# Moving the output matmuls, the convolution and the weight loads inside a fused conv and ELU-FFN kernel

## The chip, the cores and the metric

The kernel runs on one core of a Trainium2 chip. The metric is the device time of one execution in microseconds (us), and a time without further remark is the median of several executions. The kernel before took 735.51 us (three runs, 735.46 to 736.42).

All runs below gave the right result. Every one was labelled fast, but for e10_xcopy1, e11_rounds_only and e13_conv_only, which ran once only, so that their state is unknown. The kernel before falls into two groups, about 735.2 to 736.4 and 737.2 to 739.0.

## The reference

```python
# attention-like part: 8 heads of 24 channels, 7 causal taps, softmax over the taps
w = exp(weight - weight.max(-1)); w = w / (w.sum(-1) + 1e-9)          # (8, 7)
x_pad = concat([zeros(B, 6, D), x], axis=1)                            # x: (8, 4096, 192)
out[b, s, h, :] = sum_k w[h, k] * x_pad[b, s + k, h, :]
# feed-forward part on the 32768 tokens
h = out.reshape(32768, 192) @ moe_w_in                                 # (192, 2048)
g = where(h > 0, h, exp(min(h, 0)) - 1)                                # ELU
return g @ moe_w_out                                                   # (2048, 192), f32
```

Every fourth block of 1024 tokens starts a new sequence, and its convolution (conv) reads six rows of zeros in place of the six tokens before.

## The kernel before

The work is cut into 32 "supers" of 1024 tokens, and each super into 16 steps. TensorE is used as two half arrays ("tiles") of 64 rows, each with its own stream. In one step each tile computes three matmuls into one bank of PSUM (an "h", 512 columns each), and some output items (192 columns each), whose number per step stands in `ROUNDS`. Then ACT takes the exp of the bank into E, POOL clamps E to 0..1, and DVE computes gT = max(E - 1, h) and so frees the bank. Six banks form a ring. Conv of later supers takes banks of that ring too; two more banks ("ops") collect the output.

```python
ROUNDS = (
    ((0, (0, 20)), (1, (1, 7, 9, 7, 8)), (0, (12,))),
    ((0, (0, 15, 7, 10)), (1, (5, 8, 6, 13))),
)
WCOLS = ((0, 256), (256, 768), (768, 1280), (1280, 2048))      # chunks in which w_in is loaded
CONV_AT = ((4, 1, 1, 0), (10, 1, 1, 1), (12, 2, 0, 0), (15, 2, 0, 1))   # (step, supers ahead, group, half)
EARLY_CONV = ((6, 1, 0, 0), (7, 1, 0, 1), (8, 1, 1, 0), (9, 1, 1, 1), (11, 2, 0, 0), (12, 2, 0, 1))
X_PAD, X_COPY, X_LOAD = 8, 1, 15        # steps at which POOL pads, POOL copies x, SP loads xg
# ... cut ...
# PE, ahead of a conv group
if m == 0:
    W(s_tm, 1)                          # the tap matrix Tm is there
for part in range(2):
    x_ready(W, s, part)
W(s_z, z_need[s])                       # the zeros ahead of a new sequence are there
wait_bank()
# ... cut ...
# POOL: one stream, in order
load_w_in(0, (0, 1)); load_w_in(1, (0, 1)); load_x(1, 0); load_w_in(2, (0, 1))
load_x(1, 1); load_w_in(3, (0, 1)); load_x(2, 0); load_x(2, 1)
g.dma_start(w_out...)
for n in range(NP):
    s, i = divmod(n, NQ)
    if i == X_PAD and s + 2 < NS and (s + 2) % SPB == 0:
        pad_x(s + 2)                    # memset of six rows of xg
    if i == X_COPY and s and s + 3 < NS:
        copy_x(s + 3)
    if n == X_LATE[0]:
        copy_x(3)
    for u in range(2):
        W(s_exp, 2 * n + u + 1)
        g.tensor_scalar(E..., ALU.min, ALU.max)
# ... cut ...
# DVE, after its part of the setup and ahead of every gT
W(s_band, 48)                           # Tr, the band of taps, has landed
v.tensor_copy(Tm[:], Tr[:, :, ::-1]).then_inc(s_tm)
for x_, op in enumerate(steps):
    ...                                 # gT = max(E - 1, h)
```

Of the kernel before, what the change touches and what calls it, by code (L numbers as in the profile page):

```python
# [14 lines left out]
FC = 128  # L15
# [15 lines left out]
NG3 = 2  # L31
LAG = -4
ROUNDS = (
    ((0, (0, 20)), (1, (1, 7, 9, 7, 8)), (0, (12,))),
    ((0, (0, 15, 7, 10)), (1, (5, 8, 6, 13))),
)
WCOLS = ((0, 256), (256, 768), (768, 1280), (1280, 2048))
Q_PART = (0,) * 2 + (1,) * 4 + (2,) * 4 + (3,) * 6
WARM = (9, 1)

CONV_AT = ((4, 1, 1, 0), (10, 1, 1, 1), (12, 2, 0, 0), (15, 2, 0, 1))
EARLY_CONV = ((6, 1, 0, 0), (7, 1, 0, 1), (8, 1, 1, 0), (9, 1, 1, 1), (11, 2, 0, 0), (12, 2, 0, 1))
M_NS, R_NS, C_NS = 215.8, 82.5, 102.5
QUAD = 4
XTW = 136
HALO = 2
X_PAD, X_COPY, X_LOAD = 8, 1, 15
X_LATE = (13, 22)


def bass_lightweight_conv__then__act_elu_kernel(
# [37 lines left out]
    for t in range(NS):  # L89
        for half, stretches in enumerate(ROUNDS):  # L90
            n, at = NQ * (t + 1) + LAG + 8 * half, [0, 0]
            for turned, sizes in stretches:
                for size in sizes:
                    part = each[at[turned] : at[turned] + size]
                    at[turned] += size
                    rounds_at.setdefault(n, []).extend(
                        (t, half, q, kb, turned ^ (t % 2)) for q, kb in part
                    )
                    n += 1
            assert at == [len(each)] * 2  # L100
# [43 lines left out]
    for n in range(NP):  # L144
        s, i = divmod(n, NQ)
        convs = [(ahead, g, b) for at, ahead, g, b in EARLY_CONV if at == n]
        convs += [
            (s + ahead, g, b)
            for at, ahead, g, b in CONV_AT
            if at == i and s + ahead < NS  # L150
            and (s + ahead, g, b) not in [e[1:] for e in EARLY_CONV]
        ]
        for u in range(2):
            rt = 1 - u
            beside = [
                ("c", 2 * cs + g - 2, b, u, hh)
                for cs, g, b in convs
                for hh in range(HB)
            ]
            if n < first_round:  # L160
                beside += [("w", rt)] * WARM[1]
            beside += [single(item, rt) for item in rounds_at.get(n, ())]
            if rt and n in turns_at:
                beside.insert(0, ("h", n, 1, 0))
            put(u, [("h", n, u, j) for j in range(u and n in turns_at, 3)])
            put(rt, beside)
        if n % 2:
            at[:] = [max(at)] * 2
# [9 lines left out]
            left[acc_of(op)] = left.get(acc_of(op), 0) + 1  # L178
    for x_, op in enumerate(steps):
        if op[0] in "hc" and not any(op[3:]):  # L180
            take_bank(op[:3])
        elif op[0] == "o":
            acc = acc_of(op)
            if acc not in lastly:
                begins.add(x_)
                if acc[:2] == (last, 1):
                    take_bank(("l",) + acc)
            elif steps[lastly[acc]][2] != op[2]:
                ends_run[lastly[acc]] = 0
            lastly[acc] = x_  # L190
            left[acc] -= 1
            if not left[acc]:
                ends_run[x_] = 0
                final[acc] = x_
# [21 lines left out]
    with ExitStack() as stack:  # L216
# [35 lines left out]
        H = psum("H", [P, 3, 2 * GS])  # L252
        ops = psum("ops", [P, 2, GS])

        s_w = [sema(f"s_w{i}") for i in range(5)]
        s_wd = sema("s_wd")
        s_xl = [sema(f"s_xl{i}") for i in range(2)]
        s_xh = sema("s_xh")
# [67 lines left out]
            return H[:, (0, 2, 1)[j], GS * r : GS * r + GS // 2]  # L326

        def bank_of(what):
            k = turn_of[what]
            return H[:, k // 2, GS * (k % 2) : GS * (k % 2 + 1)]  # L330

# [55 lines left out]
        def _gpsimd(g: bass.BassGpSimd):  # L387
# [27 lines left out]
            def load_w_in(k, halves):  # L415
# [27 lines left out]
            load_w_in(0, (0, 1))  # L443
            load_w_in(1, (0, 1))
            load_x(1, 0)
            load_w_in(2, (0, 1))
            load_x(1, 1)
            load_w_in(3, (0, 1))
            load_x(2, 0)
            load_x(2, 1)  # L450
            g.dma_start(
                w_out.rearrange("p (q r) d -> p q (r d)", r=2), moe_w_out.rearrange("(q p r) d -> p q (r d)", p=FC, r=2)
            ).then_inc(s_w[4], 16)
            for n in range(NP):
                s, i = divmod(n, NQ)
                if i == X_PAD and s + 2 < NS and (s + 2) % SPB == 0:
# [158 lines left out]
        def _tensor(pe):  # L615
# [75 lines left out]
            for x_, op in enumerate(steps):  # L691
                if op[0] == "w":
                    rt = op[1]
                    pe.matmul(  # L694
                        ops[:, rt, :],
                        zw[HP * rt : HP * (rt + 1), 0:P],
                        zw[HP * rt : HP * (rt + 1), :],
                        start=True,
# [3 lines left out]
                elif op[0] == "c":  # L702
# [5 lines left out]
                    elif hh == 0:  # L708
                        if m == 0:
                            W(s_tm, 1)  # L710
                        for part in range(2):
                            x_ready(W, s, part)
                        W(s_z, z_need[s])
                        wait_bank()
                    n1 = BN // HB
                    h = 4 * u + HB * b + hh
                    ins = pe.matmul(  # L717
# [11 lines left out]
                elif op[0] == "h":  # L729
# [5 lines left out]
                    if j == 0:  # L735
# [5 lines left out]
                        w_in[  # L741
                            HP * r : HP * (r + 1),
                            j,
                            2 * FC * (q // 2) + q % 2 : 2 * FC * (q // 2 + 1) : 2,
                        ],
                        att[HP * r : HP * (r + 1), s % 2, j, 0:GS],
                        start=(j == 0),
# [5 lines left out]
                else:  # L753
                    _, item, rt, g = op
                    t, half, q, kb, turned = item
                    acc = acc_of(op)
                    W(s_w[4], 16)
                    W(s_tt, 2 * (NQ * t + q) + g + 1)
                    at_end = acc[:2] == (last, 1)
                    if x_ in begins:  # L760
                        if at_end:
                            wait_bank()
                        elif acc in previous:
                            taken(W, previous[acc])
                    elif steps[seen[acc]][2] != rt:
                        W(s_swap[1 - rt], ends_run[seen[acc]])
                    seen[acc] = x_
# [107 lines left out]
```

## Time and profile before

| | before |
|---|---|
| median of runs | 735.51 us |
| span of the profiled run, granted TensorE clock | 734.2 us, 1.000 |
| first h matmul of step 0 | 11.59 us |
| super 0, super 1 | 23.06, 22.48 us |
| one steady super (supers 3 to 28) | 22.25 us |
| work of one tile in a super | 21.74 us |

"Super to super" here and below is the distance between the starts of the first h matmul of two supers, read from the trace. A step starts with its first h matmul, counting six to a step in order of time. The prediction shows the totals, the waits and the windows of before; its windows, and those of after further down, were all set 0.31 us later than the steps that they are named for, which changes no length. Lines of a timeline give start us, us, engine, line, operation, [idle before and releaser]. This is the group of the conv matmuls (line, engine, operation, output<-inputs, shapes, count | busy us, mean ns | idle time of the engine just before, and its releaser):

```profile
L717 PE MATMUL H<-xg,Tm 64*128 64x240 bf16 x496 | 90.6, 263 | 1.1 <-DVE gT L605 1.1
```

Conv costs PE nearly no waiting in the kernel before. And this is DVE's timeline at the start (start us, us, engine, line, operation, [idle before and releaser]):

```profile
12.19 0.55 DVE L591 COPY Tm<-Tr 128x1024 bf16<-128x1024 bf16 x1
14.11 0.69 DVE L605 SCALAR_TENSOR_TENSOR gT<-E,H 128x512 f16<-128x512 f32 x1 [1.36 <-POOL E L464]
```

The copy of the tap matrix has no bracket: Tr had landed before DVE came to it. It is over before POOL hands DVE its first E.

### The profile page before, as it was taken

To read this page: it belongs to the slowest core of one execution; us is meant where nothing else is said; L and a number is where in the kernel's file an instruction comes from. 1 tells how busy PE (TensorE), PEld (TensorE's weight loads), DVE (VectorE), ACT (ScalarE), POOL (GpSimd) and SP (SyncE) were. 2 spreads that over 40 slices of the span, in tenths; PEclk is the share of its full clock that TensorE was granted. 3 is DMA by queue.
4 is the path that set the end of the run, shared out by engine and by line. 5 is a ranking of instruction groups with operands and counts; after the bars stand their busy time and mean duration, and the time that the engine had idled before them with its cause. 6 is when DMAs were issued, how large, how long until landed. Compare 5 with 4: busy or idle time off the path is not lost.

```text
span 734.2 us, 28751 instructions
## 1 busy us (share of the span) xinstructions
PE 726.9 (99%) x11878; PEld 653.8 (89%) x11878; DVE 655.4 (89%) x1044; ACT 675.9 (92%) x1286; POOL 637.4 (87%) x1080
## 2 busy tenths in 40 slices
PE   9899999999999999999999999999999999999998
PEld 4599899999989999999998999998998999899997
DVE  5899999999999899899999999999999999999995
ACT  5899999999999999999999999999999999999994
POOL 8889888889888888888898888898888898888894
PEclk9999999999999999999999999999999999999999
DMA  9742444333543424443424443334435334432112
GB/s 172 116 116 69 114 104 99 98 82 78 115 101 85 112 65 98 114 93 94 94 67 114 114 94 93 90 71 114 104 82 112 72 90 115 93 93 69 38 54 67
DMA packets 130303, 69.12 MB, mean 94 GB/s; under 512 B 93996, under 2 KB 129324, under 8 KB 129708
## 3 DMA queue, kind: packets, MB, share of 16 engines
q1 hardware_dynamic: 123596, 52.04, 26.9%
q0 software_dynamic: 6288, 14.75, 12.5%
q8 instruction: 93, 1.52, 0.9%
q10 hardware_dynamic: 288, 0.49, 0.2%
q14 instruction: 38, 0.31, 0.1%
HBM read 43.51 MB, written 36.57 MB: 109 GB/s over the span
## 4 chain that ended last, share of the span: by engine, by line
PE 95%; DVE 2%; POOL 1%; ACT 1%; issue 1%; ACTq 0%
PE ops L771 49%; PE H L739 41%; PE H L717 3%; DVE gT L605 2%; POOL E L464 1%; PE H L771 1%; PE ops L633 1%; ACT E L536 0%; PE H L677 0%; PE ops L677 0%; PE H L657 0%; ACT csb L514 0%; POOL x_cast L410 0%; PE H L644 0%; POOL x_cast L407 0%
## 5 line engine op out<-in xcount | busy, mean ns | idle before, releaser
L605 DVE SCALAR_TENSOR_TENSOR gT<-E,H 128x512 f16<-128x512 f32 x1024 | 649.1, 683 | 63.4 <-POOL E L464 53.0
L464 POOL TENSOR_SCALAR E<-E 128x512 f32<-128x512 f32 x1024 | 611.1, 616 | 85.5 <-ACT E L536 80.0
L739 PE MATMUL H<-att,w_in 64*128 64x512 bf16 x3072 | 633.2, 376 | 1.7 <-DVE gT L605 1.2
L536 ACT ACTIVATE E<-H 128x512 f32<-128x512 f32 x1024 | 587.4, 603 | 40.1 <-PE H L739 24.6
L771 PE MATMUL ops<-w_out,gT 64*128 64x192 f16 x8064 | 616.9, 243 | 0.0
L771 PEld LDWEIGHTS ops<-w_out,gT 64*128 64x128 f16 x8064 | 538.8, 94 | 18.4 <-PE ops L771 16.5
L739 PEld LDWEIGHTS H<-att,w_in 64*128 64x128 bf16 x3072 | 257.4, 94 | 37.1 <-DVE gT L605 14.5
L717 PE MATMUL H<-xg,Tm 64*128 64x240 bf16 x496 | 90.6, 263 | 1.1 <-DVE gT L605 1.1
L514 ACT ACTIVATE csb<-H 128x480 bf16<-128x480 f32 x124 | 72.9, 588 | 0.0
L506 ACT ACTIVATE osb<-ops 128x384 f32<-128x384 f32 x125 | 61.9, 495 | 7.3 <-PE ops L771 5.9
L717 PEld LDWEIGHTS H<-xg,Tm 64*128 64x128 bf16 x496 | 45.4, 93 | 15.9 <-issue 1.3
L410 POOL DMA_DIRECT2D x_cast<-in_x_dram x29 | 15.4, 530 | 0.0
L694 PE MATMUL ops<-zw 64*128 64x512 bf16 x24 | 8.8, 376 | 0.0
L771 PE MATMUL H<-w_out,gT 64*128 64x192 f16 x128 | 6.4, 243 | 0.0
L771 PEld LDWEIGHTS H<-w_out,gT 64*128 64x128 f16 x128 | 5.7, 94 | 0.0
L418 POOL DMA_DIRECT2D w_in<-in_moe_w_in_dram x8 | 5.2, 660 | 0.3 <-DMA wh<-in_weight_dram 0.3
L633 PE MATMUL ops<-zw 128*128 128x512 bf16 x9 | 4.0, 628 | 1.2 <-DVE zw L546 1.2
L597 DVE COPY osb<-ops 128x384 f32<-128x384 f32 x1 | 0.6, 557 | 4.2 <-PE ops L771 4.2
L633 PEld LDWEIGHTS ops<-zw 128*128 128x128 bf16 x9 | 1.2, 139 | 3.2 <-issue 2.0
L391 POOL DMA_DIRECT2D xg<-in_x_dram x4 | 3.9, 982 | 0.0
L582 DVE CAST att<-H 128x512 bf16<-128x512 f32 x1 | 0.7, 692 | 3.1 <-PE H L677 3.1
L677 PE MATMUL H<-xT,Dg 64*128 64x256 bf16 x32 | 2.6, 326 | 0.0
(47 smaller groups left out, 27.4 us busy)
## 6 DMA issues: line engine op xcount, KB each, us to landing
out_dram<-osb SPq DMA_DIRECT2D x126, 192.0 KB, 2.4
x_cast<-in_x_dram POOLq DMA_DIRECT2D x29, 384.0 KB, 4.6
xg<-x_cast SPq DMA_DIRECT2D x58, 192.0 KB
xg<-x_cast SPq DMA_DIRECT2D x58, 26.2 KB
xg<-in_x_dram POOLq DMA_DIRECT2D x4, 240.0 KB, 10.3
w_in<-in_moe_w_in_dram POOLq DMA_DIRECT2D x4, 192.0 KB, 6.5
w_out<-in_moe_w_out_dram POOLq DMA_DIRECT2D x1, 768.0 KB, 14.4
w_in<-in_moe_w_in_dram POOLq DMA_DIRECT2D x2, 288.0 KB, 10.0
```

The source lines that it names most:

```text
L410: g.dma_start(xb[s * SUP : (s + 1) * SUP, :].rearrange("(p t) d -> p (t d)", p=P), x_flat[s * SUP : (s + 1) * SUP, :].rearrange("(p t) d - ...
L418: g.dma_start(w_in[HP * r : HP * (r + 1), :, c0:c1], moe_w_in.rearrange("(p j) f -> p j f", j=3)[:, :, c0:c1],).then_inc(s_w[k], 16)
L464: g.tensor_scalar(out=E[:, n % NE, u, :], in0=E[:, n % NE, u, :], scalar1=1.0, scalar2=0.0, op0=ALU.min, op1=ALU.max,).then_inc(s_clp)
L506: a.activation(*out_pieces(acc), ACT.Copy).then_inc(s_oev)
L514: return a.activation(csb[:, s % 2, :].rearrange("p (j v h i) -> p h j v i", j=3, v=2 * WPG, h=HEADS)[:, h0 : h0 + HB], bank_of(("c", m, b ...
L536: a.activation(E[:, n % NE, u, :], bank_of(op[:3]), ACT.Exp).then_inc(s_exp)
L605: v.scalar_tensor_tensor(out=gT[:, s % NG3, q, u, :], in0=E[:, n % NE, u, :], scalar=1.0, in1=bank_of(op[:3]), op0=ALU.subtract, op1=ALU.m ...
L633: pe.matmul(ops[:, 0, :], zw[:, 0:P], zw[:], start=True, stop=True)
L694: pe.matmul(ops[:, rt, :], zw[HP * rt : HP * (rt + 1), 0:P], zw[HP * rt : HP * (rt + 1), :], start=True, stop=True, tile_position=(HP * rt ...
L717: ins = pe.matmul(bank_of(op[:3])[:, n1 * hh : n1 * (hh + 1)], Tm[HP * rt : HP * (rt + 1), h, :], xg[HP * rt : HP * (rt + 1), s % NXB, :, ...
L739: ins = pe.matmul(bank_of(op[:3]), w_in[HP * r : HP * (r + 1), j, 2 * FC * (q // 2) + q % 2 : 2 * FC * (q // 2 + 1) : 2,], att[HP * r : HP ...
L771: ins = pe.matmul(to[:, d0 : d0 + D], gT[HP * rt : HP * (rt + 1), t % NG3, q, g, t0 : t0 + P], w_out[HP * rt : HP * (rt + 1), q, :], start ...
```

## The change

The intent has four parts: other counts of output items per step and other stretches, so that fewer steps are short at the wrong place; conv and the copy of x at other steps; conv of super 1 in the two output banks, which are idle at the start, so that the ring keeps six banks; and w_in loaded in two chunks, with runs of 1 and 3 KB, in place of four chunks with runs of 0.5 to 1.5 KB, and w_out with longer runs and ahead of the x of super 2.

```diff
 ROUNDS = (
-    ((0, (0, 20)), (1, (1, 7, 9, 7, 8)), (0, (12,))),
-    ((0, (0, 15, 7, 10)), (1, (5, 8, 6, 13))),
+    ((0, (0, 11, 10)), (1, (10, 6, 6, 10)), (0, (11,))),
+    ((0, (0, 15, 8, 9)), (1, (6, 6, 7, 13))),
 )
-WCOLS = ((0, 256), (256, 768), (768, 1280), (1280, 2048))
-Q_PART = (0,) * 2 + (1,) * 4 + (2,) * 4 + (3,) * 6
+RUN = 4
+WCOLS = ((0, 512), (512, 2048))
+Q_PART = (0,) * 4 + (1,) * 12
-CONV_AT = ((4, 1, 1, 0), (10, 1, 1, 1), (12, 2, 0, 0), (15, 2, 0, 1))
-EARLY_CONV = ((6, 1, 0, 0), (7, 1, 0, 1), (8, 1, 1, 0), (9, 1, 1, 1), (11, 2, 0, 0), (12, 2, 0, 1))
+CONV_AT = ((0, 1, 1, 0), (4, 1, 1, 1), (9, 2, 0, 0), (12, 2, 0, 1))
+EARLY_CONV = ((7, 1, 0, 0), (8, 1, 0, 1), (9, 1, 1, 0), (10, 1, 1, 1), (13, 2, 0, 0), (14, 2, 0, 1))
+OPS_CONV = 2
-X_PAD, X_COPY, X_LOAD = 8, 1, 15
-X_LATE = (13, 22)
+X_PAD, X_COPY, X_LOAD = 8, 3, 15
+X_LATE = (13, 18)
@@ a conv of the first super takes no bank of the ring
-            take_bank(op[:3])
+            if op[0] == "h" or op[1] >= OPS_CONV:
+                take_bank(op[:3])
@@ bank_of
+            if what[0] == "c" and what[1] < OPS_CONV:
+                return ops[:, what[2], :]
@@ POOL, the loads
             load_w_in(0, (0, 1))
             load_w_in(1, (0, 1))
             load_x(1, 0)
-            load_w_in(2, (0, 1))
             load_x(1, 1)
-            load_w_in(3, (0, 1))
+            g.dma_start(w_out ..., r=RUN).then_inc(s_w[2], 16)
             load_x(2, 0)
             load_x(2, 1)
@@ PE, conv
-                        wait_bank()
+                        if m >= OPS_CONV:
+                            wait_bank()
+                        elif m:
+                            W(s_ce, 2 * (m - 1) + b + 1)
```

Cut: the semaphores' numbers, the stride with which PE reads w_in, the warming matmuls (6 steps in place of 12, and to the other output bank), one more wait of the second early conv, and the waits of the first output item on its bank.

More of the change, by code (lines that the diff above doesn't have):

```diff
@@ L33 @@
 ROUNDS = (
-    ((0, (0, 20)), (1, (1, 7, 9, 7, 8)), (0, (12,))),
-    ((0, (0, 15, 7, 10)), (1, (5, 8, 6, 13))),
-)
-WCOLS = ((0, 256), (256, 768), (768, 1280), (1280, 2048))
-Q_PART = (0,) * 2 + (1,) * 4 + (2,) * 4 + (3,) * 6
+    ((0, (0, 11, 10)), (1, (10, 6, 6, 10)), (0, (11,))),
+    ((0, (0, 15, 8, 9)), (1, (6, 6, 7, 13))),
+)
+RUN = 4
+WCOLS = ((0, 512), (512, 2048))
+Q_PART = (0,) * 4 + (1,) * 12
 WARM = (9, 1)
-CONV_AT = ((4, 1, 1, 0), (10, 1, 1, 1), (12, 2, 0, 0), (15, 2, 0, 1))
-EARLY_CONV = ((6, 1, 0, 0), (7, 1, 0, 1), (8, 1, 1, 0), (9, 1, 1, 1), (11, 2, 0, 0), (12, 2, 0, 1))
+CONV_AT = ((0, 1, 1, 0), (4, 1, 1, 1), (9, 2, 0, 0), (12, 2, 0, 1))
+EARLY_CONV = ((7, 1, 0, 0), (8, 1, 0, 1), (9, 1, 1, 0), (10, 1, 1, 1), (13, 2, 0, 0), (14, 2, 0, 1))
+OPS_CONV = 2
+FIRST = {}
 M_NS, R_NS, C_NS = 215.8, 82.5, 102.5
@@ L91, in bass_lightweight_conv__then__act_elu_kernel @@
             n, at = NQ * (t + 1) + LAG + 8 * half, [0, 0]
+            if t == 0 and half in FIRST:
+                n, stretches = FIRST[half]
             for turned, sizes in stretches:
@@ L159, in bass_lightweight_conv__then__act_elu_kernel @@
             ]
-            if n < first_round:
+            if n + 1 < EARLY_CONV[0][0]:
                 beside += [("w", rt)] * WARM[1]
@@ L253, in bass_lightweight_conv__then__act_elu_kernel @@
         ops = psum("ops", [P, 2, GS])
-        s_w = [sema(f"s_w{i}") for i in range(5)]
+        s_w = [sema(f"s_w{i}") for i in range(3)]
         s_wd = sema("s_wd")
@@ L445, in _gpsimd @@
             load_x(1, 0)
-            load_w_in(2, (0, 1))
             load_x(1, 1)
-            load_w_in(3, (0, 1))
+            g.dma_start(
+                w_out.rearrange("p (q r) d -> p q (r d)", r=RUN),
+                moe_w_out.rearrange("(q p r) d -> p q (r d)", p=FC, r=RUN),
+            ).then_inc(s_w[2], 16)
             load_x(2, 0)
             load_x(2, 1)
-            g.dma_start(
-                w_out.rearrange("p (q r) d -> p q (r d)", r=2), moe_w_out.rearrange("(q p r) d -> p q (r d)", p=FC, r=2)
-            ).then_inc(s_w[4], 16)
             for n in range(NP):
@@ L694, in _tensor @@
                     pe.matmul(
-                        ops[:, rt, :],
+                        ops[:, 1 - rt, :],
                         zw[HP * rt : HP * (rt + 1), 0:P],
@@ L710, in _tensor @@
                             W(s_tm, 1)
+                            if b:
+                                W(s_cv, 1)
                         for part in range(2):
@@ L743, in _tensor @@
                             j,
-                            2 * FC * (q // 2) + q % 2 : 2 * FC * (q // 2 + 1) : 2,
+                            RUN * FC * (q // RUN) + q % RUN : RUN * FC * (q // RUN + 1) : RUN,
                         ],
@@ L756, in _tensor @@
                     acc = acc_of(op)
-                    W(s_w[4], 16)
+                    W(s_w[2], 16)
                     W(s_tt, 2 * (NQ * t + q) + g + 1)
@@ L764, in _tensor @@
                             taken(W, previous[acc])
+                        else:
+                            W(s_ce, 2 * (OPS_CONV - 1) + g + 1)
                     elif steps[seen[acc]][2] != rt:
```

## The prediction

> **What bounds the kernel now.** I read the engine totals first, then the groups, then the waits, then windows cut at the kernel's own stages, and last the start times of the single matmuls in the trace. Engines, and the groups that make up their time (line, engine, operation, output<-inputs, shapes, count | busy us, mean ns | idle before, releaser):
>
> ```profile
> PE 726.9 (99%) x11878; PEld 653.8 (89%) x11878; DVE 655.4 (89%) x1044; ACT 675.9 (92%) x1286; POOL 637.4 (87%) x1080
> ...
> L605 DVE SCALAR_TENSOR_TENSOR gT<-E,H 128x512 f16<-128x512 f32 x1024 | 649.1, 683 | 63.4 <-POOL E L464 53.0
> L464 POOL TENSOR_SCALAR E<-E 128x512 f32<-128x512 f32 x1024 | 611.1, 616 | 85.5 <-ACT E L536 80.0
> L739 PE MATMUL H<-att,w_in 64*128 64x512 bf16 x3072 | 633.2, 376 | 1.7 <-DVE gT L605 1.2
> L536 ACT ACTIVATE E<-H 128x512 f32<-128x512 f32 x1024 | 587.4, 603 | 40.1 <-PE H L739 24.6
> L771 PE MATMUL ops<-w_out,gT 64*128 64x192 f16 x8064 | 616.9, 243 | 0.0
> ```
>
> PE looks full, but its matmuls use half the rows (64*128), so two streams ("tiles") run side by side and PE counts as busy when only one of them works. Idle time must be counted per tile. The weight loads show it: they stop while a tile cannot go on.
>
> ```profile
> PEld H L739 <- DVE gT L605: 14.5, 44, 0.7
> PEld H L739 <- issue: 9.6, 31, 0.4
> ```
>
> 31 times is once for each super of 1024 tokens but one, and DVE (gT) is what frees the H banks. So some 24 us lie in short, regular stops. The start times confirm it. On one tile, starts follow each other by 215.8 ns (h matmul, 512 columns), 82.5 ns (output matmul) and 102.5 ns (conv matmul). A super has 96, 256 and 16 of them, half on each tile: 48 x 215.8 + 128 x 82.5 + 8 x 102.5 = 21.74 us. The trace takes 22.25 us from super to super (supers 3 to 28). Each tile loses 0.51 us. Placing every matmul on its tile, in program order, the loss sits in few places: at step 0 of the 16 steps (tile 0 idle 0.26, tile 1 0.16 just before it), at step 4 (0.25 and 0.18), and 0.06 on tile 1 at each of the three places where the output runs swap tiles.
>
> The start is different. Windows: steps 0 to 5 of super 0, steps 6 to 12, steps 13 to 15, then two steady supers (us; then PE, PEld, DVE, ACT, POOL busy with counts, clock, DMA share, GB/s):
>
> ```profile
> 11.90:18.84 6.94, 6.61 (x49) 2.12 (x45) 5.58 (x10) 6.06 (x13) 5.97 (x11) 1.00 1.30 193
> 18.84:30.70 11.86, 9.73 (x84) 4.08 (x85) 10.02 (x17) 9.76 (x21) 8.90 (x15) 1.00 0.86 136
> 30.70:34.96 4.26, 4.26 (x79) 4.05 (x76) 3.04 (x5) 3.54 (x8) 4.07 (x8) 1.00 0.59 95
> 235.47:257.73 22.26, 22.25 (x373) 20.28 (x369) 20.35 (x33) 21.08 (x41) 19.71 (x35) 1.00 0.39 95
> 257.73:279.98 22.25, 22.24 (x373) 20.33 (x370) 20.31 (x33) 21.07 (x41) 19.60 (x34) 1.00 0.39 95
> ```
>
> Six steps take 6.94 us at first: DVE starts follow at 598 ns, two to a step, 1.196 us. The next seven take 11.86, and DVE, which was solid, stands still between single operations:
>
> ```profile
> 17.70 4.38 DVE L605 SCALAR_TENSOR_TENSOR gT<-E,H 128x512 f16<-128x512 f32 x7
> 22.35 0.69 DVE L605 SCALAR_TENSOR_TENSOR gT<-E,H 128x512 f16<-128x512 f32 x1 [0.27 <-POOL E L464]
> 23.19 0.69 DVE L605 SCALAR_TENSOR_TENSOR gT<-E,H 128x512 f16<-128x512 f32 x1 [0.15 <-POOL E L464]
> ```
>
> That is a round trip: conv takes H banks out of the ring of six there, and PE waits for a bank that DVE has not freed.
>
> **What the Trainium skill says.** "TensorE: Matmul & The Clock Gate", section Back-to-back issue gap: a warm gap is N/2.4 + 2.5 ns. That gives 215.8 and 82.5; the trace agrees exactly. "TensorEngine Tiling (Array Packing)", Key Properties: different tiles run weight loads and matmuls in parallel; the trace agrees, an h stream and an output stream keep their own spacing side by side. "Perfetto Trace Analysis", Identifying Performance Opportunities: the same bubble repeating on the engine that should be full can mean that PSUM has no room for the next tile; the stops at steps 0 and 4 are this. "Perfetto Trace Analysis", Optimizing DMA Performance: large descriptors matter; in the trace a packet of 512 B (at the target) took 65 ns, 1024 B 110, 1536 B 135, so this agrees too.
>
> **The change, part by part.** No matmul of the real work goes; 12 of 24 warming ones do, and they lie beside waiting.
>
> *Steady supers.* A step's time on a tile is 647 ns (three h) + 82.5 per output item + 205 with a conv. By step 0 to 15, items before: 9 7 8 12 0 15 7 10 5 8 6 13 0 20 1 7, conv at 4, 10, 12, 15. After: 6 6 10 11 0 15 8 9 6 6 7 13 0 11 10 10, conv at 0, 4, 9, 12. The sum stays 21.74. An h bank is ready again 2.05 us after its matmuls end where nothing queues (ACT 0.60, POOL 0.62, DVE 0.69, hand-overs 0.15), plus 0.06 for PE to notice. A conv in the ring shortens it from six to five.
> Step 0 before: the first h needs the bank of step 13's second h, because the conv of step 15 sits in between. It has steps 14 and 15 only, 0.73 + 1.43 without the stall; its h ends about 0.18 into step 14, so 1.98 against some 2.2 needed (a wait for att comes on top). After: no conv within six takes, so the bank is that of step 13's first h; steps 13 to 15 (1.55, 1.47, 1.47) less 0.81 give 3.7 us. This stop should go.
> Step 4 before: the second h needs step 2's first, 1.31 - 0.81 + 1.64 + 0.20 = 2.34, while that bank took 2.53 + 0.06, because POOL issues the x_cast copy (0.53 us) in step 1 and is behind by 0.5 from there. After: 1.47 - 0.81 + 1.55 + 0.20 = 2.43 against 2.11, since the copy now comes in step 3, whose long step absorbs it. This one should go too.
> The new tight places by the same working: step 12's second h, 2.34 against 2.31 (a conv copy in ACT's queue), and step 14's second, 2.43 against 2.41 (two output copies in ACT's queue). So the stops are gone by a hair, and I count 0.0 to 0.1 for these. The swaps stay three a super, 3 x 0.06 = 0.17 on tile 1, and the tiles keep in step. Loss 0.17 to 0.30 in place of 0.51: 0.21 to 0.34 a super, over 28 supers 6 to 9.5; about 0.5 more in the last three.
>
> *Start.* Conv of super 1 writes the output banks, idle until step 13, so the ring keeps six banks and DVE its 1.196: steps 6 to 12 take 7 x 1.196 = 8.4 in place of 11.86. ACT has two exps and a conv copy in four of them, 0.477 + 0.45 + 0.477 = 1.41 a step, 0.2 over DVE's pace; four times is 0.8, of which its lead of some 0.5 hides most: 8.7. Steps 13 to 15 get two convs and three items more, 1.76 + 1.68 + 1.47 = 4.91 in place of 4.26, of which the items (0.25) come off later. Gain 11.86 + 4.26 - 8.7 - 4.91 + 0.25 = 2.8.
>
> *Loads.* First data on this queue at 4.3 us. Before, 1.57 MB (target) of w_in shared the way with xg. Now w_in comes first: the first chunk at about 150 KB/us 2.6 us, the second at about 200 KB/us 5.9: landed near 14 us, needed by step 4 at 16.4. xg of super 1 follows near 18, needed at 20; w_out near 23, needed at 27. Nothing on the path either way, and the first h (11.6) waits for the conv of super 0, not for weights.
>
> Sum: 6 to 9.5, + 0.5, + 2.8 = 9.3 to 12.8, middle 11: 735.5 - 11 = **724.5 us**.
>
> **Rivals.** (a) Step 12 or 14 becomes the new stop: margins of 0.02 to 0.03 are below my accuracy, and without the old stops PE comes earlier everywhere. If 0.2 comes back a super, 730. For: step 14's second h was already waiting before. Against: both windows are no shorter than the time needed. (b) The big w_in chunk makes xg late: conv at step 7 would stop PE by 1 to 2 us, total near 726. For: the DMA share was above 1 until 24 us. Against: 2 us of margin. (c) The swap cost hides too, or steps are fully even: period 21.74, another 5 us, 720. For: tile 1 has some slack. Against: each swap idles already now. (d) Another engine is the limit: DVE needs 32 x 0.598 = 19.1 of 21.9, ACT 15.3 + 1.8 + 1.5 = 18.6. No.
>
> **Range and chances.** (a) and (b) together reach 730, (c) 720.5. 2% is 14.7 us, thus 720.8: only (c) reaches it. Slower by 2% would need half a microsecond more per super; nothing in the ledger gives that. Faster 0.11, within 0.88, slower 0.01.
>
> **What would show it.** Right: super to super near 21.95; no weight-load stop marked "issue" once a super; the DVE group's stretch from 18 to 27 us solid; step 13 starting near 27.5. Wrong: a period of 22.1 or more with weight loads waiting for DVE near steps 12 to 14; PE waiting near 20 us for a DMA; a first h later than 12 us.

## The result, and the profile after

The changed kernel took 734.29 us (four runs, 733.24 to 735.55), beside 735.58 for before. The ratio is 0.9981, with a 95% interval of 0.9958 to 1.0003. All ratios here are the mean time of one kernel's fast runs over that of the other's of the same rounds, so they are not quite the ratio of the medians. The gain is some 1 us where the prediction had 11; the time lies above the predicted range. All outputs are right.

The page of the kernel after, engine totals and groups:

```profile
PE 717.8 (98%) x11866; PEld 640.9 (87%) x11866; DVE 652.7 (89%) x1044; ACT 657.2 (90%) x1286; POOL 630.5 (86%) x1076
...
L612 DVE SCALAR_TENSOR_TENSOR gT<-E,H 128x512 f16<-128x512 f32 x1024 | 646.5, 683 | 59.9 <-POOL E L471 51.2
...
L751 PE MATMUL H<-att,w_in 64*128 64x512 bf16 x3072 | 612.2, 379 | 5.1 <-DVE gT L612 4.3
...
L729 PE MATMUL H<-xg,Tm 64*128 64x240 bf16 x480 | 87.6, 262 | 4.1 <-POOL xg L410 3.8
```

The h matmuls now wait 5.1 us where they waited 1.7, and conv 4.1 where it waited 1.1. A new releaser stands there: POOL's memset of xg, line 410, the pad. The waits of the kernel after (engine, line waited for: us in total, times, longest us):

```profile
PEld H L751 <- DVE gT L612: 7.6, 8, 4.2
...
DVE Tm L598 <- DMA Tr<-conv_taps: 5.7, 1, 5.7
...
PE H L751 <- DVE gT L612: 4.3, 3, 3.7
PE H L729 <- POOL xg L410: 3.8, 7, 0.6
```

Both of before's repeated stops are gone from this list: weight loads stopped for DVE 8 times in place of 44, and the "issue" stop of 31 times is not there. In their place stand a single stop of 5.7 us (DVE waits for the DMA that brings Tr), with 3.7 us of PE behind it, and a stop that comes seven times. Seven is the number of sequences after the first, and each needs one pad.

The windows show both in the same terms as the prediction's: steps 0 to 5 of super 0, steps 6 to 12, steps 13 to 15, a super without the pad, the next with it (us; then PE, PEld, DVE, ACT, POOL busy with counts, clock, DMA share, GB/s; again each 0.31 us late):

```profile
11.26:22.80 11.54, 7.86 (x50) 4.65 (x48) 6.08 (x11) 5.93 (x11) 5.93 (x10) 0.74 1.27 205
22.80:31.54 8.74, 8.05 (x60) 3.84 (x56) 7.75 (x13) 8.40 (x19) 7.41 (x13) 0.96 0.25 30
31.54:37.93 6.39, 5.70 (x94) 4.90 (x95) 5.18 (x9) 5.15 (x11) 5.77 (x11) 1.00 0.79 133
212.55:234.47 21.92, 21.92 (x373) 19.79 (x369) 20.21 (x33) 20.39 (x42) 19.44 (x34) 1.00 0.48 94
234.47:257.11 22.64, 22.09 (x373) 19.75 (x369) 20.36 (x33) 20.48 (x42) 19.63 (x35) 1.00 0.51 99
```

Steps 0 to 5 took 11.54 us in place of 6.94, with a granted clock of 0.74. A plain super takes 21.92 in place of 22.25, and every fourth one 22.64.

The chain of work from 3.6 us on (start us, us, what) says what the first steps waited for:

```profile
3.61 3.64 DMA conv_taps<-zt
...
7.27 9.02 DMA Tr<-conv_taps
...
16.31 0.43 DVE Tm L598
16.74 0.61 DVE gT L612
```

The band of taps goes out to DRAM and comes back as Tr; it took until 16.29. DVE's copy of it stands ahead of every gT, so no bank was freed before. PE had filled its six banks by about 13.7 and stood until 17.39. The windows of 2 us after it show what came on top:

```profile
18.00:20.00 2.00, 2.00 (x12) 1.38 (x12) 2.00 (x4) 1.11 (x2) 0.43 (x1) 0.50 1.23 208
20.00:22.00 2.00, 2.00 (x12) 1.41 (x10) 1.59 (x4) 1.29 (x3) 1.51 (x4) 0.50 1.29 203
```

The clock (third number from the end) was halved for some 6 us after a gap of 3.7 us on PE: steps 3, 4 and 5 took 1.69, 1.71 and 1.71 us each instead of about 1.20. The Trainium skill, "TensorE: Matmul & The Clock Gate", Part 1, puts the fall to half speed after an idle window of about 3.4 us; this trace agrees (gap 3.7, clock 0.50). Later runs don't: in e8_trim, e5_tm_later and e14_newloads_tm_act the clock also fell to half, and PE's longest stop before it was 1.86, 2.01 and 2.46 us.

The pad, in POOL's timeline of super 2, and the conv matmul that waited for it in PE's:

```profile
71.42 0.62 POOL L471 TENSOR_SCALAR E<-E 128x512 f32<-128x512 f32 x1 [0.19 <-ACT E L543]
71.97 0.25 POOL L410 MEMSET xg<- 6x192 bf16 x1
72.20 1.18 POOL L471 TENSOR_SCALAR E<-E 128x512 f32<-128x512 f32 x2
```

```profile
72.48 0.26 PE L729 MATMUL H<-xg,Tm 64*128 64x240 bf16 x1 [0.55 <-POOL xg L410]
```

POOL does one thing after the other. The pad for step 8 comes after the E of step 7, which ACT hands over about a step late; PE, with conv now at step 9, was already there.

Where the time of the profiled runs went, with two later kernels beside it:

| us | before | after | e3_both | e9_tm_act |
|---|---|---|---|---|
| first h matmul at | 11.59 | 10.95 | 9.90 | 10.01 |
| super 0 | 23.06 | 26.67 | 22.80 | 22.48 |
| super 1 | 22.48 | 21.74 | 21.74 | 21.74 |
| supers 2 to 30 | 644.31 | 640.24 | 635.10 | 635.10 |
| super 31 and the end | 32.76 | 33.45 | 33.21 | 32.96 |
| span | 734.2 | 733.0 | 722.8 | 722.3 |

So 3.6 us were lost in super 0. Supers 2 to 30 won 4.1 us where 9.2 were there to win: the missing 5.1 us are the seven supers with a pad, 7 x (22.64 - 21.91). The first h of before came unusually late in this one trace: e6_steady_only below has the setup and the loads of before unchanged, and had it at 10.01 (and super 0 took 24.06 there). With the new loads it came at 10.44 to 11.20 in the profiles, after a wait of 0.40 to 1.35 us for the first chunk of w_in; with the old loads, this trace apart, at 9.57 to 10.01. The end of the program became 0.2 to 0.7 us longer. That goes with the new early conv: after the last output copy, every profile with it took 3.19 to 3.87 us to the end, and every one without it 2.77 to 2.80. Why is not known.

### The profile page after: what moved, and what is told of

Same layout as the page of the kernel before. It is cut to its first block, busy times and chain, and to the rows that moved or that the text cites. A ratio compares the mean times of both kernels' runs of the same rounds, so it can differ in the third digit from the quotient of the medians.

```text
span 733.0 us, 28722 instructions
## 1 busy us (share of the span) xinstructions
PE 717.8 (98%) x11866; PEld 640.9 (87%) x11866; DVE 652.7 (89%) x1044; ACT 657.2 (90%) x1286; POOL 630.5 (86%) x1076
## 4 chain that ended last, share of the span: by engine, by line
PE 94%; DMA 2%; ACT 2%; POOL 1%; issue 1%; DVE 0%; ACTq 0%
PE ops L785 50%; PE H L751 40%; PE H L729 3%; DMA Tr<-conv_taps 1%; ACT E L543 1%; POOL E L471 1%; PE H L785 1%; DMA conv_taps<-zt 0%; DVE gT L612 0%; POOL xg L410 0%; ACT L484 0%; ACT csb L521 0%; PE ops L701 0%; POOL x_cast L415 0%; POOL x_cast L418 0%
## 5 line engine op out<-in xcount | busy, mean ns | idle before, releaser
L543 ACT ACTIVATE E<-H 128x512 f32<-128x512 f32 x1024 | 566.8, 613 | 58.3 <-PE H L751 53.8
L751 PE MATMUL H<-att,w_in 64*128 64x512 bf16 x3072 | 612.2, 379 | 5.1 <-DVE gT L612 4.3
L785 PE MATMUL ops<-w_out,gT 64*128 64x192 f16 x8064 | 594.6, 243 | 0.0
L785 PEld LDWEIGHTS ops<-w_out,gT 64*128 64x128 f16 x8064 | 523.7, 94 | 41.6 <-PE ops L785 26.2
L751 PEld LDWEIGHTS H<-att,w_in 64*128 64x128 bf16 x3072 | 293.1, 111 | 20.3 <-DVE gT L612 7.6
L729 PE MATMUL H<-xg,Tm 64*128 64x240 bf16 x480 | 87.6, 262 | 4.1 <-POOL xg L410 3.8
L729 PEld LDWEIGHTS H<-xg,Tm 64*128 64x128 bf16 x480 | 39.7, 94 | 19.0 <-issue 6.6
L701 PE MATMUL ops<-zw 64*128 64x512 bf16 x12 | 5.7, 502 | 0.0
L729 PE MATMUL ops<-xg,Tm 64*128 64x240 bf16 x16 | 3.0, 265 | 0.4 <-ACT csb L521 0.3
```

Of the source, the lines that this page charges most:

```text
L543: a.activation(E[:, n % NE, u, :], bank_of(op[:3]), ACT.Exp).then_inc(s_exp)
L701: pe.matmul(ops[:, 1 - rt, :], zw[HP * rt : HP * (rt + 1), 0:P], zw[HP * rt : HP * (rt + 1), :], start=True, stop=True, tile_position=(HP ...
L729: ins = pe.matmul(bank_of(op[:3])[:, n1 * hh : n1 * (hh + 1)], Tm[HP * rt : HP * (rt + 1), h, :], xg[HP * rt : HP * (rt + 1), s % NXB, :, ...
L751: ins = pe.matmul(bank_of(op[:3]), w_in[HP * r : HP * (r + 1), j, RUN * FC * (q // RUN) + q % RUN : RUN * FC * (q // RUN + 1) : RUN,], att ...
L785: ins = pe.matmul(to[:, d0 : d0 + D], gT[HP * rt : HP * (rt + 1), t % NG3, q, g, t0 : t0 + P], w_out[HP * rt : HP * (rt + 1), q, :], start ...
```

## The experiments

My theory: the steady gain came, and two faults ate it. The first is the pad in POOL's stream, 5.1 us. The second is the new order and size of the loads, which delays Tr and with it every gT, some 4 us. The rivals were that the long supers come from something else with a period of four; that the start is lost through the conv in the output banks and not the loads; and that the loss is DVE waiting for Tr alone, or the weights alone.

### Undoing the two faults: e1_pad5, e2_oldloads, e3_both, e4_before_newloads

These four ran together. Before took 735.28, 735.55, 735.65 and 738.36, 738.96, 738.99, 739.03 beside them (median 738.36).

e1_pad5 changes one number of the changed kernel, so that the pad stands three steps earlier.

```diff
-X_PAD, X_COPY, X_LOAD = 8, 3, 15
+X_PAD, X_COPY, X_LOAD = 5, 3, 15
```

> The changed kernel with one number different: the memset that pads xg for the first super of a sequence stands in POOL's stream at step 5 of 16, not step 8. Theory A: in the changed kernel the conv of step 9 waits for this memset (period 22.64 us in every fourth super against 21.91 in the others, 7 times 0.73), so all periods become 21.9 and the time falls by 5.1 us, from 734.3 to about 729.2. Rival: the longer period comes from something else that repeats every four supers (the load of x for the next sequence landing late); then POOL would stop at step 5 instead, and the time stays at 734 or rises.

It took 729.16 us (728.29 to 729.94), ratio 0.988. All steady supers took 21.91, the former long ones too, and the line of the pad has gone from PE's waits. POOL's timeline of super 2 has the memset earlier:

```profile
67.26 0.25 POOL L410 MEMSET xg<- 6x192 bf16 x1
```

That is 5.1 us less than after, as seven times 0.73. Super 0 still took 26.17. The pad is settled, and it is separate from the start.

e2_oldloads keeps the pad at 8 and puts back w_in in four chunks and the order of the loads.

```diff
-RUN = 4
-WCOLS = ((0, 512), (512, 2048))
-Q_PART = (0,) * 4 + (1,) * 12
+RUN = 2
+WCOLS = ((0, 256), (256, 768), (768, 1280), (1280, 2048))
+Q_PART = (0,) * 2 + (1,) * 4 + (2,) * 4 + (3,) * 6
@@ loads on POOL: w_in(0), w_in(1), x(1, 0), w_in(2), x(1, 1), w_in(3), x(2), w_out
```

> The changed kernel with the weight loads of the kernel before (w_in in four chunks among the x loads, w_out with two rows to a run). Theory B: in the changed kernel the big packets of w_in starve the small load Tr (landed 9 us after issue), whose copy stands on DVE ahead of all gT; PE then ran dry and its clock fell to half. With the old loads DVE's first gT starts near 14 us, the clock stays at 1.0, super 0 takes about 20.5 us in place of 26.7, and the time falls by some 6 us to 728.5. Rival: the start was lost to the conv of super 1 in the output banks, or to x arriving late for it; then super 0 stays above 25 us and the time near 734.

It took 731.47 us (730.17 to 733.40), ratio 0.9917. Super 0 fell from 26.67 to 22.88, the clock was 1.000, and every fourth super kept its 22.64. So the conv in the output banks is not what cost the start; the loads are. But 6 us and a super 0 of 20.5 were expected: the size was missed by half.

e3_both is both edits together.

> Both of the edits above in one kernel. If theories A and B are right and independent, the savings add: 734.3 - 5.1 - 6 = 723.2 us, close to what was predicted for the change. If one hides the other, over 727.

It took 725.65 us (724.87 to 728.44), ratio 0.9843. The repairs add up, with a little over: counted from after, 5.1 and 2.8 us alone, 8.6 together. (After ran in an earlier round, so these are differences across rounds; the traces by themselves give the 5.1.)

e4_before_newloads is the kernel before with only the new chunks and order of the loads.

> The kernel before with only the new weight loads (w_in in two chunks ahead of x, w_out with four rows to a run). Theory B: the first gT on DVE starts 2.5 us later or more and the clock drops once, so the time rises by 3 to 5 us, to about 739. Rival (the loads are harmless, the rest of the change lost the start): 735.5.

It took 739.86 us (739.36 to 740.30), ratio 1.0028 against all seven runs of before and 4.3 us more than the faster group's 735.5. Super 0 took 26.32 and the first gT came at 15.68. The loads do the damage in the old kernel just as well.

### Which part of the start: e5_tm_later, e6_steady_only, e7_start_only, e8_trim

Before took 735.51 and six times 737.24 to 738.99 beside these (median 738.51).

e5_tm_later leaves the new loads and the pad, and moves DVE's copy of Tr behind the gT of steps 0 to 2.

```diff
-            W(s_band, 48)
-            v.tensor_copy(Tm[:], Tr[:, :, ::-1]).then_inc(s_tm)
             for x_, op in enumerate(steps):
@@ in the branch of an h
+                    if (n, u) == (3, 0):
+                        W(s_band, 48)
+                        v.tensor_copy(Tm[:], Tr[:, :, ::-1]).then_inc(s_tm)
```

> The changed kernel, its new loads kept, with DVE's copy of Tr moved behind the gT of steps 0 to 2 (the conv that needs it runs at step 7). Theory B says that the load Tr is late because of the big packets, but costs time only because its copy stands ahead of all gT on DVE. Then DVE's first gT starts near 13 us, PE never runs dry and the clock stays at 1.0; super 0 falls from 26.7 to about 22.5 us and the time from 734.3 to about 730. Rival: w_in's late second chunk or late x holds the start; then super 0 stays above 25 us.

It took 732.52 us, ratio 0.9917; super 0 fell to 24.20 and the first gT came at 12.73. The rest of the loss did not go, because the next thing was late too. PE's timeline:

```profile
16.92 0.41 PE L752 MATMUL H<-att,w_in 64*128 64x512 bf16 x1 [2.01 <-DMA w_in<-in_moe_w_in_dram]
```

Step 4 waited for the second chunk of w_in, three quarters of the matrix behind one semaphore. So the fault of the loads is two delays, one behind the other: Tr, then the large chunk. The clock fell to 0.5 here too.

e6_steady_only is the kernel before with the new counts, conv steps and copy, and the pad at 5; start and loads are the old ones.

```diff
 ROUNDS = (
-    ((0, (0, 20)), (1, (1, 7, 9, 7, 8)), (0, (12,))),
-    ((0, (0, 15, 7, 10)), (1, (5, 8, 6, 13))),
+    ((0, (0, 11, 10)), (1, (10, 6, 6, 10)), (0, (11,))),
+    ((0, (0, 15, 8, 9)), (1, (6, 6, 7, 13))),
 )
-CONV_AT = ((4, 1, 1, 0), (10, 1, 1, 1), (12, 2, 0, 0), (15, 2, 0, 1))
+CONV_AT = ((0, 1, 1, 0), (4, 1, 1, 1), (9, 2, 0, 0), (12, 2, 0, 1))
-X_PAD, X_COPY, X_LOAD = 8, 1, 15
-X_LATE = (13, 22)
+X_PAD, X_COPY, X_LOAD = 5, 3, 15
+X_LATE = (13, 18)
```

> The kernel before with only the steady part of the change (new rounds, conv places, copy and late load of x) and the pad memset at step 5; its own loads and its own start. The period should be 21.91 us in place of 22.25, super 0 as before (23.1): 735.5 - 29 x 0.34 = 725.6 us. Rival: the steady gain needs the new start; then the period stays above 22.1.

It took 727.58 us, ratio 0.9858, in two pairs: 725.83 and 726.02, 729.15 and 729.20. Steady supers took 21.91. The lower pair lies 9.5 us under the faster group of before: nearly the whole gain is in the steady supers.

e7_start_only is the kernel before with the early conv in the output banks alone (`EARLY_CONV`, `OPS_CONV = 2` and the shorter warming).

> The kernel before with only the new start (conv of super 1 in the output banks at steps 7 to 10, conv of super 2 at steps 13 and 14, fewer warming matmuls). As predicted for the change the start would gain 2.8 us: 732.7. From the run with both edits I now expect less: 3 us are won up to step 13 and most is given back at steps 13 to 15, where conv of super 2 takes banks of the ring while DVE still sets the pace: about 734.5.

It took 737.85 us (734.90 to 738.23), ratio 0.9982, which decides little about the start's worth: its profiled run, and two more of the four, fell into the slower of the two groups. (The fast one, 734.90, lies 0.6 us under the one fast run of before, 735.51.) It did show what that group is. DVE's and POOL's timelines of that run:

```profile
12.63 3.40 DVE L599 COPY Tm<-Tr 128x1024 bf16<-128x1024 bf16 x1 [1.97 <-DMA Tr<-conv_taps]
```

```profile
12.23 3.51 POOL L472 TENSOR_SCALAR E<-E 128x512 f32<-128x512 f32 x6
```

The same copy took 0.55 us in the profile of before and 0.43 in that of after. Here it took 3.40 us, and it ended 0.3 us after POOL ran out of work. The Trainium skill, "SBUF — State Buffer", section Who interferes with whom, says that DVE, in a mode that uses two ports, and GpSimd (POOL) hold a shared pair of ports exclusively, the first for its whole instruction, and that the one that comes second is fully blocked. The trace agrees in that the copy was blocked (that it runs in such a mode is not shown here): it came 0.4 us after POOL had begun an unbroken row of six, and got through only when the row was over. I call this the port race (theory C): whether DVE's copy or POOL's row comes first at the start would decide into which group a run falls.

Other traces limit this theory. e11_rounds_only, further down, shows the same hold: its copy came 0.63 us after the row had begun and took 3.16 us. But in e6_steady_only the copy came second too, 0.17 us after the row had begun at 12.38, and was over long before the row, which ran on to 19.62:

```profile
12.55 0.82 DVE L591 COPY Tm<-Tr 128x1024 bf16<-128x1024 bf16 x1 [1.90 <-DMA Tr<-conv_taps]
```

It was over 0.34 us after the end of the one POOL instruction that ran when it came, and POOL's next took 0.88 us in place of some 0.6. In e8_trim below the copy came in the middle of a row and took 0.66 us. So coming second is not enough for the long hold; what else decides is not known.

e8_trim is e3_both with DVE's copy later as in e5, and with POOL's copy of x for super 3 issued before step 0, where e3 has it in step 13.

```diff
+            copy_x(3)
             for n in range(NP):
@@
-                if n == X_LATE[0]:
-                    copy_x(3)
```

> The kernel with both edits (old loads, pad at step 5), and two more: the copy of Tr behind the gT of steps 0 to 2 on DVE, and the first x_cast copy issued by POOL ahead of step 0, not at step 13, where its two issues held POOL for 1.1 us and left DVE idle 0.95 us. Expected: 0.75 us less at step 2 and about 0.7 less at steps 13 to 15, so 1.2 to 1.5 us under the run with both edits. Rival: PE is not held by DVE there, no difference.

The expectation failed: 727.55 us (725.85 to 729.50), ratio 0.9852, no better than e3_both. The chain of its start shows why:

```profile
12.30 0.53 POOL x_cast L416
12.83 0.51 POOL x_cast L419
13.34 0.67 POOL E L472
```

The two issues stand on the way to the first E now, and the first gT came at 14.03 after 3.6 us of idle DVE. At the place where they were taken away they did help, by the 0.7 us that had been expected there: steps 13 to 15 of super 0 took 5.65 us, against 6.35 in e3_both. But steps 0 to 5 took 9.41 against 7.70, and the clock fell to 0.54 in the window from 16 to 18 us. The two issues cost POOL 0.5 us each in both places, and at the start more hung on them.

### The copy on another engine, and which part makes the steady gain: e9_tm_act, e10_xcopy1, e11_rounds_only, e12_before_tm_act

Before took 735.26, 735.35, 735.81, 736.36 and 738.13, 738.58, 738.60 beside these (median 736.36).

e9_tm_act is e3_both with the copy of Tr on ACT, behind its exps of steps 0 to 2, so that neither DVE nor the shared ports stand in the way.

```diff
                     ).then_inc(s_exp)
+                    if (n, u) == (2, 1):
+                        W(s_band, 48)
+                        a.activation(Tm[:], Tr[:, :, ::-1], ACT.Copy).then_inc(s_tm)
```

> The kernel with both edits (old loads, pad at step 5), with the copy of Tr given to ACT, after its exps of steps 0 to 2. Theory C: DVE's 16-bit copy and POOL's stream want the same SBUF ports; in a slow start the copy begins a moment after POOL's first op and holds DVE until POOL runs dry (3.40 us in place of 0.55), PE then idles and its clock halves. On ACT no such race is left: the clock stays at 1.0 and all runs lie within 1 us, near 724.2 (0.75 us less than the good runs of the kernel with both edits). Rival: the slow runs come from elsewhere (clock or DMA); then two groups some 3 us apart remain.

It took **724.72 us** (724.50, 724.64, 724.80, 726.43), ratio 0.9846 with an interval of 0.9816 to 0.9876. This is the best kernel, ahead of both given ones. Super 0 took 22.48. The copy took 1.10 us on ACT, and DVE began at 12.98 with nine gT in a row:

```profile
12.98 5.47 DVE L614 SCALAR_TENSOR_TENSOR gT<-E,H 128x512 f16<-128x512 f32 x9 [2.33 <-POOL E L472]
```

e10_xcopy1 is e3_both with `X_COPY = 1` in place of 3, one look.

> The kernel with both edits, with the x_cast copy issued in step 1 again, as in the kernel before, not in step 3. By the working of the prediction the second h of step 4 then waits (2.53 + 0.06 needed, 2.43 there), some 0.16 us a super: period 22.05 to 22.1 us. Rival: the place of the copy does not matter, period 21.91.

It took 733.56 us and a super 22.21, 0.30 more than e3_both, where I had expected 0.16. The stop at step 4 came back (0.30 on one tile, 0.46 on the other), and with it the weight loads' wait for DVE:

```profile
PEld H L752 <- DVE gT L613: 18.6, 43, 1.4
```

So the copy in step 3 is needed; the stop came back where the prediction's working puts it, at about twice the size.

e11_rounds_only is the kernel before with the new counts alone, one look.

> The kernel before with only the new counts of output items per step; conv, copy and loads as before. The stop at step 0 should go, since steps 14 and 15 are then 1.47 and 1.68 us long (2.97 against 2.2 needed), and the stop at step 4 should shrink to 0.16 (as in the run above): period 22.07 us. If the new places of conv are what counts, 22.25.

This expectation failed: 749.12 us. The run had the slow start (super 0 27.15), but the steady super took 22.61 as well, 0.36 more than before. The stop at step 0 was gone, that at step 4 stayed, and a new one of 0.5 stood at step 15. There the new counts put the swap of the output tiles, whose h takes its bank ahead of the conv of the same step; the conv then takes the bank of step 13's first h, about 2.43 us after that h ended, while that bank was free only 2.93 after.

e12_before_tm_act is the kernel before with the copy of Tr on ACT.

> The kernel before with only the copy of Tr given to ACT, after its exps of steps 0 to 2. The kernel before has shown two groups of times, 735.5 and 738.5 to 739, with a granted clock of 1.0 and 0.995 to 0.998. Theory C: the second group is the same race in the start; with the copy on ACT only the fast one is left, near 735 or up to 1 us under it. Rival: the groups stay, as they do in the kernel before in the same rounds.

It took 735.33 us (735.06 to 736.03). All four runs lie in the faster group, where four of before's seven did. That would happen by luck in (4/7)^4, about 11%. It supports the port race and does not prove it.

### Conv alone, and the remains of the start: e13_conv_only, e14_newloads_tm_act, e15_ops3

Before took 735.18, 735.22, 735.26, 735.60 and 738.49, 738.60, 738.61 beside these (median 735.60).

e13_conv_only is the kernel before with the new conv steps (and the pad at 5) but old counts and `X_COPY = 1`, one look.

> The kernel before with only the new places of conv (and what they need: pad at step 5, the late x load at step 18); counts of output items and the x_cast copy in step 1 as before. Counts alone made the period worse (22.61 us). If the gain needs both, this one lies at 22.25 or above; if conv's places are the gain, at 22.0 or below.

It took 738.62 us, a super 22.36. So counts alone (22.61), conv steps alone (22.36) and the two without the copy (22.21) each leave or make a stop; only all three gave 21.91. The copy in step 3 by itself was not run.

e14_newloads_tm_act is the changed kernel with the pad at 5 and the copy of Tr on ACT: the new loads with all else of e9.

> The changed kernel (new loads) with pad at step 5 and the copy of Tr on ACT. The race is gone, so what is left of the start's loss against the same kernel with the old loads (724.7) is the loads' own: step 4 waits for w_in's second chunk until some 17.2 us. Expected: super 0 at 24 us in place of 22.5, time near 726.5. If the loads cost nothing by themselves: 724.7. If the copy on ACT now holds ACT's exps until Tr lands at 16 us: 729, as with DVE.

It took 728.12 us (726.75 to 728.93), ratio 0.9881, 3.4 us more than e9_tm_act. The chain of its start has the second chunk of w_in in it:

```profile
4.55 13.42 DMA w_in<-in_moe_w_in_dram
...
18.02 1.00 PE H L752 x3
```

It landed at 17.97, where the prediction had it near 14. ACT's exp of step 3 was also held until 17.57 by its copy, since Tr had landed at about 16.3. So the new loads hurt through both, and this run does not part the two. It does show that the loss is the loads' own and not that of the engine on which the copy stands.

e15_ops3 is e9_tm_act with half of super 2's conv in the output banks too, and the early convs at steps 6 to 11.

```diff
-EARLY_CONV = ((7, 1, 0, 0), (8, 1, 0, 1), (9, 1, 1, 0), (10, 1, 1, 1), (13, 2, 0, 0), (14, 2, 0, 1))
-OPS_CONV = 2
+EARLY_CONV = ((6, 1, 0, 0), (7, 1, 0, 1), (8, 1, 1, 0), (9, 1, 1, 1), (10, 2, 0, 0), (11, 2, 0, 1))
+OPS_CONV = 3
```

> The best kernel so far (both edits, copy of Tr on ACT, 724.7), with the first conv of super 2 in the output banks too and all six early convs at steps 6 to 11. Steps 13 to 15 then have no conv in the ring: by PE's work 4.5 us, against 6.96 measured. ACT has two more conv copies ahead of step 12, which gives some back. Expected 1 to 2 us less: 723.2. If the loss there is DVE's and POOL's and not the ring's: 724.7.

It took 724.96 us (724.49 to 725.94): no gain over e9_tm_act. Steps 13 to 15 fell from 6.33 to 5.42 us and super 0 by 0.57 to 21.91, but super 1 rose by 0.32 to 22.06 and the end by 0.54.

## Why the prediction was right or wrong, point by point

**Steady supers: right in mechanism and size, but one wait was missed.** Both stops went, the tight steps 12 and 14 held (rival a did not come), the swaps cost 0.17 a super (rival c did not come), and the super took 21.91, at the better edge of the predicted loss of "0.17 to 0.30". Supers 2 to 30 of e3_both won 9.2 us by the trace; the prediction had 6 to 9.5 for 28 of them.

The failing step is in the ledger of the conv moves. The prediction checked the conv of step 9 for its bank, and not for its data. It names `X_COPY` and the ring, and no sentence of it has the pad. The PE code waits for `s_z` ahead of `wait_bank`, and the memset that raises it stood at step 8 of POOL's stream. With conv at step 12 there were four steps between; with conv at step 9 there was one, and POOL runs about one step behind PE. This gave 7 x 0.73 = 5.1 us. e1_pad5 is the proof: one number moved, and 5.1 us came back.

**Loads: wrong.** The step that failed is "Nothing on the path either way, and the first h (11.6) waits for the conv of super 0, not for weights." The first chunk of w_in was to take 2.6 us from 4.3 on, so to be there by 6.9; the first h waited 0.76 us for it, until 10.95. That cost little. What cost much is that the prediction looked only at the loads that the change touches. The two small transfers that carry the taps to DRAM and back run at the same time on another queue. In the traces of after, e1 and e4, with the new loads, the first took 3.64 to 3.88 us from issue and the second 7.64 to 9.02; with the old ones the first took 2.19 to 2.33 (e6, e7, e11) and the second 5.98 to 6.96 (the seven profiles in which DVE waited for it). And DVE's copy of the result is first in line before the work of all engines. On top of it, the second chunk landed at 17.97 (e14) and not near 14: the estimate's 200 KB/us was too high for what else was under way. Then the halved clock made the gap longer. e2, e4 and e14 show that the loads did it; e5 shows that there were two delays in series. Rival (b), that "the big w_in chunk makes xg late", had the right cause and the wrong victim. By e1 to e3 it cost 2.8 to 3.5 us, and by e4 4.3.

**Start: right in direction, mis-sized.** Steps 6 to 12 took 8.74 us in after and 8.75 in e3_both; predicted was 8.7, in place of 11.86. But steps 13 to 15 were summed as PE's work, 4.91. They took 6.39 in after and 6.35 in e3_both. (Counted from the first h matmul of step 13 itself, which starts 0.6 us earlier there, they took 6.98 and 6.97.) The conv of super 2 takes ring banks there, and POOL spends 1.1 us on two issues. POOL's and DVE's timelines of e3_both:

```profile
28.70 0.58 POOL L415 DMA_DIRECT2D x_cast<-in_x_dram  x1
29.28 0.51 POOL L418 DMA_DIRECT2D x_cast<-in_x_dram  x1
```

```profile
30.48 2.48 DVE L613 SCALAR_TENSOR_TENSOR gT<-E,H 128x512 f16<-128x512 f32 x4 [0.95 <-POOL E L472]
```

DVE stood 0.95 us behind these. e8_trim puts the two issues at 0.7 us. What the start is worth is best read from e3_both against e6_steady_only, which has the same steady part and the same loads, the old start, and its first h as early (9.90 and 10.01). Super 0 took 22.80 us against 24.06 and super 1 21.74 against 21.96, so 1.5 us were won, and the end took 0.65 more. The faster runs of the two, from different rounds, lie 0.95 apart. So the term "Gain ... = 2.8" was worth about 1.5 us up to super 2 and about 0.9 in the whole program; the term of the sum that failed is the 4.91.

**The sum.** With both faults taken out (e3_both) the kernel takes 725.65 us, and with the copy on ACT 724.72, where 724.5 was predicted. That nearness is partly luck: the missing 2 us of the start are made up by the steady part, which came at its better edge.

**Two readings in the prediction.** The 24 us of its "short, regular stops" are waits of the weight loads; the time that a tile lost was 0.51 us a super, some 16 us. And the formula that it takes from "TensorE: Matmul & The Clock Gate", section Back-to-back issue gap, stands there for a single matmul; for a stream at 512 columns that section gives about 131 ns. On one tile of this kernel the stream kept 215.8 ns, so here the measurement is with the formula.

**Left open.** Why some runs fall into the slower group is not settled. The port race (theory C) has two traces that show the long hold (e7 and e11: 3.40 and 3.16 us for a copy of 0.55), one in which the copy came second and was not held (e6), and two kernels that avoid it, wholly (e12) or nearly (e9). It can't be all: the changed kernel falls in two pairs as well (733.2 and 735.4), and in the trace of the slower one Tr came only when POOL's row was over. What the 726.43 of e9 was is not known, nor how much of the loads' loss is Tr and how much the large chunk, nor why the end of the program grew with the new early conv.

## What to carry to other kernels

When an operation is moved earlier, list everything it waits for, with the engine and the place in that engine's stream that raises each semaphore, and not only the buffer that the move is about; a wait that was four steps early can be none. When loads are made larger or reordered, look at every transfer that is under way then, on all queues, and at what stands in line behind the smallest of them. And check whether the work of the new places has companions there: counts, conv places and copy gave 0.34 us a super together, 0.04 without the copy, and a loss with the counts or the conv places alone.

## What the Trainium skill lacked or had wrong

- "DMA: Bandwidth & Descriptors" says how an engine takes turns between queues, but gives no sense of what that does to a small load beside a large one. Here, Tr (256 KB) landed 9.02 us after its issue beside the new 3 KB runs of w_in, and in the kernel before, issued at 5.90, it had landed by 12.19, so in 6.3 us at most (5.98 to 6.96 in seven other runs with the old loads).
- "TensorE: Matmul & The Clock Gate" has the halved clock, as cited above, after an idle window of about 3.4 us. Here PE's longest stop before the fall was 1.86 us (e8), 2.01 (e5), 2.46 (e14) and 3.21 to 3.68 (e1, e4, e7, e11 and after). What the halved clock does to a kernel with three engines in a ring is on no page that I read: a step took 1.7 us in place of 1.2, for some 6 us, after a single gap of 3.7.
- "TensorEngine Tiling (Array Packing)" has no cost for handing an accumulation from one row tile to the other. Here it was 0.06 us on one tile at each of three swaps, 0.17 us a super, in before and after alike.
- "SBUF — State Buffer" says that the shared ports are held for the whole of one instruction. In e7 and e11 the blocked copy did not get in between POOL's instructions: it lasted 3.40 and 3.16 us, through a row of six of 0.6 us each, in place of 0.43 to 0.55. In e6 and e8 it did get in after one (0.82 and 0.66 us). The page doesn't say what decides between the two.
